# First products early, halves two blocks at once, first gates in two loads: an HGRN2 attention block with a PReLU network on one core

## The chip, the cores and the metric

The kernel runs on one core of a Trainium2 chip. A core has a matrix engine (TensorE, PE in the profile; its weight loads are listed apart, as PEld), a vector engine (VectorE, DVE), a scalar engine (ScalarE, ACT), a general engine (GpSimd, POOL) and an engine that here only issues transfers (SyncE, SP). Each works through its own queue in order and waits on semaphores that the others raise. Transfers between main memory (HBM), the on-chip memory (SBUF) and back run on 16 DMA engines that all queues share. [...]

The metric is the time of one execution on the device, in microseconds (us). A profiled execution has its own time and a span, from its first to its last instruction; the tables below and the prediction say which of these they mean.

## The reference

All is float32. With batch 4, 8 heads, 768 time steps and head width 48:

```python
f = 1 / (1 + exp(-f_logit))
state = zeros((B, H, D, D))
for t in range(S):
    state = f[:, :, t, :, None] * state + einsum('bhd,bhe->bhde', k[:, :, t], v[:, :, t])
    y[:, :, t] = einsum('bhd,bhde->bhe', q[:, :, t], state)
x = y.transpose(0, 2, 1, 3).reshape(B * S, H * D)      # 3072 x 384
h = x @ w_in                                           # 384 x 2048
g = maximum(h, 0) + alpha * minimum(h, 0)
out = g @ w_out                                        # 2048 x 384
```

So each output row of the attention is a sum over all earlier time steps of `(q . decay * k) v`, where the decay is the product of the gates `f` between the two steps. The network after it is two dense products with a PReLU between.

## The kernel before

**Tiling.** The time axis is cut into 6 chunks of 128 steps (`C`), a chunk into two halves of 64 (`CH`), those into blocks of 32 (`DB`) and those into groups of 4. Two batch elements (`U`) are worked on together. That makes 12 steps `(bp, c)`, batch pair `bp` inner and chunk `c` outer. A step's tiles hold two heads on the partitions (48 of each 64 rows, `par` 0 and 1) and batch element, head pair and time on the free axis.

**Stages of a step.** Each is a generator, and a `yield` marks where another may go on.
- `prepare` (letters P and Q; six pieces) loads `f`, `q`, `k` and `v`, takes the sigmoid (L277), and makes products: `qd` (L280, L285), `q` times the gates of 0, 1, 2 or 3 preceding steps ("lagged q"); the gates' products in a group (`kr`, `fs`), their running products (`ps`, `ss`), `k4` (L345), `us` (L312 to L342), and for whole blocks `kh`, `ks`, `q3` (L366 to L402). In steps with `c` = 0 there are also `k16` and `q16` for the pair of halves of 16 in a block of 32 (L385, L400). The sixth piece copies `q3` into `A` (L415) and, in later chunks, transposes `ks` on VectorE into `kt` (L420) and moves it with 16 transfers on SP's queue into `ksn` (L425).
- `carry` (O; two pieces) multiplies `kh` with `q3` into `off` (L442); with `c` = 0 also `k16` with `q16`, one block of 32 at a time (L452), and copies both out to `ad` (L456) and `A` (L460); with `c` = 0 TensorE transposes `ks` into `pk` (L469), copied to `ksn` (L472). The second piece multiplies `ksn` with `v` into `pd` (L482) and takes it to the carried state, which lives beside `v` in `vs` (L492, L496, or L498).
- `attend` (S) multiplies for each of the two batch elements `k` with `qd` into `raw` (L518) and `k4` with `us` into `qu` (L533), and takes the masked parts of both into `ad` by predicated copies on VectorE (L524, and L555 or L539). Then `ad` is copied into `A` (L561), `A` is multiplied with `vs` into `py` (L572), `py` is copied to `y` (L581), and `y` goes to `xT`, in the first step by products with a shifted identity (`xt`, L590, L592), later by transfers (L600).
- `network` (n) works on the 256 rows of one step: eight groups of `ph` (L614), each with the PReLU on ScalarE and VectorE (L619, L622) into `g`; then `po` (L638), copied out (L632) and stored (L634).
- The weights come as 64 bit floats and are turned to float32 in eight pieces each: a load on SP's queue into `raw` buffers (L192; four of them), upper parts on ScalarE (L197, L199; letters a and b), lead, rest and power on VectorE (L205 to L218; w and v), and a sum by a transfer that adds (L225, POOL's queue).

**What sets the order.** It is written by hand. For each pass `n` a string of letters says which generator goes on next; TensorE, VectorE and ScalarE get their instructions in exactly this order (`manual_schedule`). Pass 0 holds the first step alone, with the preparation of the second; in pass `n` the network of step `n` runs (`before`) beside the attention of step `n` + 1 and the preparation of step `n` + 2. The first four strings are in `first`, the rest of the passes use `usual`. Loads of `f`, `q` and `k` stand on POOL's queue except in the first step, where they are on SP's. A tile with one buffer is loaded anew when its last reader is done.

**PSUM.** A pool of two pairs of banks (`pair`) serves `off`, `pk`, `raw`, `qu`, `pd` and `py` in turn, a pool of four single banks (`bank`) serves `xt`, `ph` and `po`.

Of the kernel before, what the change touches and what calls it, by code (L numbers as in the profile page):

```python
# [14 lines left out]
AF = mybir.ActivationFunctionType  # L15
# [16 lines left out]
def kernel(  # L32
# [63 lines left out]
    def bank(name):  # L96
        return psn.tile([128, 512], F32, tag="net", name=name)

# [150 lines left out]
    def quads(t):  # L249
        return t.rearrange("p (n r) -> p n r", r=4)  # L250
# [5 lines left out]
    def prepare(bp, c, x):  # L256
# [5 lines left out]
        def load(name, src, bufs=2):  # L262
            t = work.tile([128, W], F32, tag=name, name=f"{name}_{i}", bufs=bufs)
            loads.dma_start(out=t.rearrange("p (u x) -> p u x", u=U),  # L264
                              in_=src[b0:b0 + U, c].rearrange("u p h t -> p u (h t)"))
            return t

        f = quads(load("f", fT, 1))
# [8 lines left out]
        nc.scalar.activation(f, f, AF.Sigmoid)  # L277
# [16 lines left out]
        yield  # L294

# [133 lines left out]

    def carry(bp, c, x):  # L430
# [3 lines left out]
        off = pair(f"off_{i}")  # L434
        for u in range(U):
            for hp in range(HP):
                for cc in range(NC2):
                    g = (u * HP + hp) * NC2 + cc
                    o = (u * HP + hp) * DB
                    for par in range(2):  # L440
                        r_ = rows(par)
                        nc.tensor.matmul(off[CH * cc:CH * cc + DB, par, o:o + DB],  # L442
                                         lhsT=kh[r_, g], rhs=q3[r_, g, 2], start=True, stop=True)
        if not c:
            for u in range(U):
                for hp in range(HP):
                    for j in range(NJ):
                        g = (u * HP + hp) * NJ + j
                        o = U * HP * DB + (u * HP + hp) * 16
                        for par in range(2):  # L450
                            r_ = rows(par)
                            nc.tensor.matmul(off[DB * j:DB * (j + 1), par, o:o + 16], lhsT=x["k16"][r_, g],  # L452
                                             rhs=x["q16"][r_, g], start=True, stop=True)
            for u in range(U):
                o = U * HP * DB + u * HP * 16
                nc.scalar.copy(ad[:, u, :, :, 16:DB], off[:, :, o:o + HP * 16].rearrange("p r (h t) -> p r h t", h=HP))  # L456
        for cc in range(NC2):
            s_ = slice(CH * cc, CH * cc + DB)
            for par in range(2):
                nc.scalar.copy(A[s_, :, par * HP:(par + 1) * HP, CH * cc + DB:CH * (cc + 1)],  # L460
                               off[s_, par, 0:U * HP * DB].rearrange("p (u h t) -> p u h t", u=U, h=HP))


        if not c:
            pk = pair(f"pk_{i}")
            for u in range(U):
                for hp in range(HP):
                    a = (u * HP + hp) * NC2
                    nc.tensor.transpose(pk[:, u, hp * 128:(hp + 1) * 128], ks[:, a:a + 2].rearrange("p c s t -> p (c s t)"), ident)  # L469
            ksn = x["ksn"] = work.tile([128, U, HP * 128], F32, tag="ksn", name=f"ksn_{i}", bufs=1)  # L470
            for u in range(U):
                nc.scalar.copy(ksn[:, u], pk[:, u])  # L472
        yield
        pd = pair(f"pd_{i}")
        ksn = x["ksn"]
        for u in range(U):
            for hp in range(HP):
                for cc in range(NC2):
                    for par in range(2):
                        o = (u * HP + hp) * D  # L480
                        s_ = halves(cc)[0]
                        nc.tensor.matmul(pd[rows(par), cc, o:o + D],  # L482
# [3 lines left out]
        def moved(cc):  # L486
# [6 lines left out]
            for par in range(2):  # L493
                now = pd[rows(par), cc, 0:U * HP * D].rearrange("p (u h e) -> p u h e", u=U, e=D)
                if c or cc:
                    nc.vector.tensor_tensor(then[:, :, par:H:2], then[:, :, par:H:2], now, ALU.add)  # L496
                else:
                    nc.scalar.copy(then[:, :, par:H:2], now)  # L498
# [5 lines left out]
    def attend(bp, c, x):  # L504

        i = f"{bp}_{c}"
        k, k4, us = (x[n] for n in ("k", "k4", "us"))


        QL, QS = (UW, UW) if c else (VW, C)  # L510
        for u in range(U):
            raw = pair(f"raw{u}_{i}")
            for hp in range(HP):
                for j in range(NJ):
                    g = (u * HP + hp) * NJ + j
                    for par in range(2):
                        r_ = rows(par)
                        nc.tensor.matmul(raw[DB * j:DB * (j + 1), par, hp * C:hp * C + QW],  # L518
                                         lhsT=k[r_, g * DB:(g + 1) * DB], rhs=qd[r_, g], start=True, stop=True)
# [8 lines left out]
            for hp in range(HP):  # L528
                for j in range(NJ):
                    g = (u * HP + hp) * NJ + j  # L530
                    for par in range(2):
                        r_ = rows(par)
                        nc.tensor.matmul(qu[DB * j:DB * (j + 1), par, hp * QS + 4:hp * QS + QL],  # L533
                                         lhsT=k4[r_, g * DB:(g + 1) * DB], rhs=us[r_, g, 4:QL], start=True, stop=True)
            if c:
# [20 lines left out]
            yield  # L556
# [49 lines left out]
    def network(bp, c, x):  # L606
# [47 lines left out]
        "P2 a P w P a P a w O P w S a w S Q a O a w S2 Q w S Q S",  # L654
        "P a w a P w2 b n2 v O n b2 v S n v n P S b S v b n S v n b v Q b n b n v O v n v Q3 S2 n2 Q2",
        "O n2 S n2 S Q S2 n3 O n Q n Q2 n S2 n Q2 n",
        "n O n2 S n2 S Q n O Q n2 S Q n S n S Q2 S Q n2",
# [78 lines left out]
```

## Time and profile before

| | us |
|---|---|
| median of 4 runs | 651.81 (649.96 to 653.48) |
| the profiled execution, its own time | 652.45 |
| its span | 650.7 |
| TensorE busy, matmuls | 607.9 |
| VectorE busy | 423.8 |
| ScalarE busy | 254.9 |
| first `ph` matmul | 51.74 |
| end of the first step's `po` | 111.28 |

The profile's page gives busy times, the span in 40 slices (16.3 us each) with the granted TensorE clock, the chain of work that ended last, and groups of instructions with the time that their engine stood idle before them and what ended it. "<-issue" after an idle time means that nothing in the profile ended it. A timeline row has start, duration, engine, line, operation, what it writes and reads, shape and count; a merged row covers several instructions. A row of a stretch has, after the stretch and its length, the busy time of PE, PEld, DVE, ACT and POOL, the granted clock (1.00 is full), the DMA engines' share and the GB/s that they moved. A matmul of float32 is counted as two instructions.

### The profile page before, as it was taken

To read this page: it belongs to the slowest core of one execution; us is meant where nothing else is said; L and a number is where in the kernel's file an instruction comes from. 1 tells how busy PE (TensorE), PEld (TensorE's weight loads), DVE (VectorE), ACT (ScalarE), POOL (GpSimd) and SP (SyncE) were. 2 spreads that over 40 slices of the span, in tenths; PEclk is the share of its full clock that TensorE was granted. 3 is DMA by queue.
4 is the path that set the end of the run, shared out by engine and by line. 5 is a ranking of instruction groups with operands and counts; after the bars stand their busy time and mean duration, and the time that the engine had idled before them with its cause. 6 is when DMAs were issued, how large, how long until landed. Compare 5 with 4: busy or idle time off the path is not lost.

```text
span 650.7 us, 17589 instructions
## 1 busy us (share of the span) xinstructions
PE 607.9 (93%) x7580; PEld 451.0 (69%) x7580; DVE 423.8 (65%) x866; ACT 254.9 (39%) x466; POOL 67.6 (10%) x114
## 2 busy tenths in 40 slices
PE   0448799999999999999999999999999999999997
PEld 0347676876876875875876876876876786786874
DVE  6879889694595686686686587577577477450220
ACT  5676782532343161361360460361351352331210
POOL 9143122000000000000000000001001000000000
PEclk9858999999999999999999999999999999999999
DMA  7989986312223213213213313313213201201000
GB/s 258 269 207 252 265 229 145 87 62 59 43 68 89 73 41 86 72 40 87 73 34 90 73 37 90 70 39 89 57 53 88 48 31 34 43 1 25 24 1 24
DMA packets 73116, 56.22 MB, mean 86 GB/s; under 512 B 47408, under 2 KB 64944, under 8 KB 73040
## 3 DMA queue, kind: packets, MB, share of 16 engines
q0 software_dynamic: 10112, 27.53, 15.9%
q1 hardware_dynamic: 57536, 25.37, 15.6%
q10 hardware_dynamic: 5392, 2.21, 1.6%
q8 instruction: 60, 0.98, 0.7%
q14 instruction: 16, 0.13, 0.1%
HBM read 36.21 MB, written 4.72 MB: 63 GB/s over the span
## 4 chain that ended last, share of the span: by engine, by line
PE 91%; DVE 4%; issue 2%; ACT 2%; DMA 1%; DVEq 0%; ACTq 0%
PE ph L614 39%; PE po L638 38%; PE py L572 3%; PE raw L518 3%; PE qu L533 3%; PE pd L482 2%; PE off L442 1%; DMA f<-in_fT 1%; PE pk L469 0%; ACT A L561 0%; PE off L452 0%; DVE us L319 0%; DVE k L345 0%; ACT us L312 0%; DVE us L342 0%
## 5 line engine op out<-in xcount | busy, mean ns | idle before, releaser
L614 PE MATMUL ph<-xT,w_in_sb 128*128 128x256 f32 x1152 | 263.6, 386 | 3.4 <-issue 3.4
L638 PE MATMUL po<-w_out_sb,g 128*128 128x384 f32 x768 | 252.9, 488 | 0.0
L614 PEld LDWEIGHTS ph<-xT,w_in_sb 128*128 128x128 f32 x1152 | 217.6, 192 | 36.9 <-issue 7.0
L638 PEld LDWEIGHTS po<-w_out_sb,g 128*128 128x128 f32 x768 | 144.9, 190 | 96.8
L622 DVE SCALAR_TENSOR_TENSOR g<-neg,om,ph 128x256 f32<-128x256 f32 x192 | 83.2, 476 | 164.3 <-ACT neg L619 164.1
L619 ACT ACTIVATE neg<-ph 128x512 f32<-128x512 f32 x96 | 57.4, 600 | 168.7 <-PE ph L614 164.2
L632 ACT COPY o<-po 128x384 f32<-128x384 f32 x24 | 11.5, 478 | 145.6 <-PE po L638 117.5
L524 DVE COPY_PREDICATED ad<-mraw,raw 128x256 f32<-128x256 int32 (+1 forms) x96 | 42.3, 441 | 7.6 <-PE raw L518 5.1
L539 DVE COPY_PREDICATED ad<-mquad,qu 128x224 f32<-128x224 int32 (+6 forms) x140 | 41.9, 299 | 6.2
L561 ACT COPY A<-ad 32x256 f32<-32x256 f32 x96 | 38.4, 400 | 2.3 <-DVE ad L539 0.9
L328 DVE TENSOR_TENSOR us<-us,fs 128x768 f32<-128x768 f32 (+5 forms) x60 | 37.2, 620 | 0.3
L312 ACT COPY us<-qd 128x256 f32<-128x256 f32 x48 | 30.2, 666 | 9.8 <-DVE qd L285 9.7
L264 POOL DMA_DIRECT2D k<-in_kT x11 | 8.3, 759 | 235.7 <-PE raw L518 208.9
L285 DVE TENSOR_TENSOR qd<-qd,f 128x768 f32<-128x768 f32 (+2 forms) x36 | 27.1, 753 | 8.2 <-ACT qd L280 8.0
L572 PEld LDWEIGHTS py<-A,vs 128*64 128x64 f32 x768 | 25.0, 145 | 10.3 <-ACT A L561 8.1
L415 ACT COPY A<-q 48x512 f32<-48x512 f32 x44 | 27.1, 616 | 9.3 <-DVE f L410 4.5
L518 PE MATMUL raw<-qd,k 48*32 48x80 f32 x1536 | 23.3, 240 | 7.9 <-issue 6.4
L572 PE MATMUL py<-A,vs 128*64 128x64 f32 x768 | 26.9, 231 | 3.9 <-ACT A L561 3.9
L518 PEld LDWEIGHTS raw<-qd,k 48*32 48x32 f32 x1536 | 18.2, 108 | 16.1 <-issue 15.4
L442 PE MATMUL off<-q,kh 48*32 48x32 f32 x768 | 9.5, 199 | 18.4 <-DVE q L366 18.4
L581 ACT COPY y<-py 128x512 f32<-128x512 f32 x24 | 12.9, 589 | 35.2 <-PE py L572 35.2
L533 PE MATMUL qu<-us,k 48*32 48x112 f32 (+1 forms) x1536 | 25.4, 259 | 0.0
(85 smaller groups left out, 437.9 us busy)
## 6 DMA issues: line engine op xcount, KB each, us to landing
w_out_raw<-in_w_out SPq DMA_DIRECT2D x8, 767.8 KB, 5.2
w_in_raw<-in_w_in SPq DMA_DIRECT2D x8, 767.2 KB, 6.0
f<-in_fT POOLq DMA_DIRECT2D x11, 512.0 KB, 4.1
q<-in_qT POOLq DMA_DIRECT2D x11, 512.0 KB, 4.0
k<-in_kT POOLq DMA_DIRECT2D x11, 512.0 KB, 4.2
out<-o SPq DMA_DIRECT2D x24, 192.0 KB, 2.0
vs<-in_v POOLq DMA_DIRECT2D x22, 192.0 KB, 3.7
w_out_sb<-w_out_lead POOLq DMA_DIRECT2D x8, 384.0 KB, 5.4
```

The lines of the kernel that those rows point to most:

```text
L312: nc.scalar.copy(q4[:, :, :, r], qdv[r][:, :, :, 0])
L328: nc.vector.tensor_tensor(us[:, :, UO[m]:UO[m] + 4 * n].rearrange("p g (i r) -> p g i r", r=4), us[:, :, skip:skip + 4 * n].rearrange("p g ...
L518: nc.tensor.matmul(raw[DB * j:DB * (j + 1), par, hp * C:hp * C + QW], lhsT=k[r_, g * DB:(g + 1) * DB], rhs=qd[r_, g], start=True, stop=True)
L524: nc.vector.copy_predicated(adu[:, :, :, d:4], mraw[:, d, :, d:4].bitcast(I32).unsqueeze(1).broadcast_to((128, H, NB, n)), rv[:, :, QO[d]: ...
L533: nc.tensor.matmul(qu[DB * j:DB * (j + 1), par, hp * QS + 4:hp * QS + QL], lhsT=k4[r_, g * DB:(g + 1) * DB], rhs=us[r_, g, 4:QL], start=Tr ...
L539: nc.vector.copy_predicated(ad[:, u, :, :, 4 * m:DB], mquad[:, lo:lo + n].bitcast(I32).unsqueeze(1).unsqueeze(1).broadcast_to((128, 2, HP, ...
L561: nc.scalar.copy(A[s_, u, :, s_], ad[s_, u].rearrange("p r h t -> p (r h) t"))
L572: nc.tensor.matmul(py[64 * par:64 * par + 64, u, o:o + CH], lhsT=vs[bp][:, cc, u, hd * D:hd * D + 64], rhs=A[:, u, par * HP + hp, CH * cc: ...
L614: nc.tensor.matmul(ph[:, j * T:(j + 1) * T], lhsT=w_in_sb[:, kt, (f + j) * 128:(f + j + 1) * 128], rhs=xT[:, kt], start=(kt == 0), stop=(k ...
L619: nc.scalar.activation(neg, phv, AF.Relu, scale=-1.0)
L622: nc.vector.scalar_tensor_tensor(g[:, j], neg[:, j], om[:, f + j:f + j + 1], phv[:, j], ALU.mult, ALU.add)
L638: nc.tensor.matmul(po[u][:, 0:DM], lhsT=gs[f // 2][:, f % 2, u * C:(u + 1) * C], rhs=w_out_sb[:, f], start=(f == 0), stop=(f == NF - 1))
```

## The change

It has four parts.

1. In the first step the load of `f` and its sigmoid are done in two halves, one for each batch element.
2. In the first step the products of `k` and lagged `q` (`raw`) move from `attend` to the end of the first piece of `prepare`, for both batch elements. `off`, `pk` and `pd` of this step take single banks in place of pairs. `attend` then does both elements' `raw` copies and `qu` products, and after them both elements' `qu` copies.
3. In steps with `c` = 0 the products of `k16` and `q16` are done for two blocks of 32 at once: half as many, each twice as wide in both directions, of which only the two diagonal blocks are used. They are copied to `ad` by eight copies in place of two.
4. The strings of the first four passes are written anew. Among other things, in the third string four pieces of the coming step's preparation are left in place of six, and the last two stand in the fourth string (its two P).

```diff
+    def two(name, begin):
+        if begin:
+            return [bank(f"{name}{k}") for k in range(2)]
+        t = pair(name)
+        return [t[:, k] for k in range(2)]
...
-        def load(name, src, bufs=2):
+        def load(name, src, bufs=2, parts=1):
             t = work.tile([128, W], F32, tag=name, name=f"{name}_{i}", bufs=bufs)
-            loads.dma_start(out=t.rearrange("p (u x) -> p u x", u=U),
-                              in_=src[b0:b0 + U, c].rearrange("u p h t -> p u (h t)"))
+            n = U // parts
+            for u in range(0, U, n):
+                loads.dma_start(out=t.rearrange("p (u x) -> p u x", u=U)[:, u:u + n],
+                                in_=src[b0 + u:b0 + u + n, c].rearrange("u p h t -> p u (h t)"))
             return t
-        f = quads(load("f", fT, 1))
+        parts = 1 if bp or c else U
+        f = quads(load("f", fT, 1, parts))
...
-        nc.scalar.activation(f, f, AF.Sigmoid)
+        for part in range(parts):
+            fp = f[:, part * W // 4 // parts:(part + 1) * W // 4 // parts]
+            nc.scalar.activation(fp, fp, AF.Sigmoid)
...
         lagged(3)
         yield
+        if not (bp or c):
+            x["raw"] = [within(i, u, k) for u in range(U)]
...
+    def within(i, u, k):
+        raw = pair(f"raw{u}_{i}")
+        for hp in range(HP):
+            for j in range(NJ):
+                g = (u * HP + hp) * NJ + j
+                for par in range(2):
+                    r_ = rows(par)
+                    nc.tensor.matmul(raw[DB * j:DB * (j + 1), par, hp * C:hp * C + QW],
+                                     lhsT=k[r_, g * DB:(g + 1) * DB], rhs=qd[r_, g], start=True, stop=True)
+        return raw
...
-                    for j in range(NJ):
-                        g = (u * HP + hp) * NJ + j
-                        o = U * HP * DB + (u * HP + hp) * 16
+                    for cc in range(NC2):
+                        g = (u * HP + hp) * NJ + 2 * cc
+                        o = at + (u * HP + hp) * DB
                         for par in range(2):
                             r_ = rows(par)
-                            nc.tensor.matmul(off[DB * j:DB * (j + 1), par, o:o + 16], lhsT=x["k16"][r_, g],
-                                             rhs=x["q16"][r_, g], start=True, stop=True)
-            for u in range(U):
-                o = U * HP * DB + u * HP * 16
-                nc.scalar.copy(ad[:, u, :, :, 16:DB], off[:, :, o:o + HP * 16].rearrange("p r (h t) -> p r h t", h=HP))
+                            nc.tensor.matmul(off[par][CH * cc:CH * (cc + 1), o:o + DB],
+                                             lhsT=x["k16"][r_, g:g + 2].rearrange("p g t -> p (g t)"),
+                                             rhs=x["q16"][r_, g:g + 2].rearrange("p g t -> p (g t)"), start=True, stop=True)
+            for par in range(2):
+                for j in range(NJ):
+                    s_ = slice(DB * j, DB * (j + 1))
+                    o = 16 * (j % 2)
+                    nc.scalar.copy(ad[s_, :, par, :, 16:DB],
+                                   off[par][s_, at:2 * at].rearrange("p (u h t) -> p u h t", u=U, h=HP)[:, :, :, o:o + 16])
...
+        if begin:
+            for stage in (first, second):
+                for u in range(U):
+                    stage(u)
+                yield
+        else:
+            for u in range(U):
+                first(u)
+                second(u)
+                yield
...
-        "P2 a P w P a P a w O P w S a w S Q a O a w S2 Q w S Q S",
-        "P a w a P w2 b n2 v O n b2 v S n v n P S b S v b n S v n b v Q b n b n v O v n v Q3 S2 n2 Q2",
-        "O n2 S n2 S Q S2 n3 O n Q n Q2 n S2 n Q2 n",
-        "n O n2 S n2 S Q n O Q n2 S Q n S n S Q2 S Q n2",
+        "P2 a P a w P2 a O w2 a O P S w S Q S a2 S w Q a w Q2 S w Q S a",
+        "b w2 n O v n S b n v S b2 v P n2 v S b v n Q b v b n S b v3 O Q n2 Q2 n S n Q S n Q",
+        "n O n2 S n2 S Q S n Q O S n3 S n Q n S n Q",
+        "n P O n2 P S n2 S Q n O Q n2 S Q n S n S Q2 S Q n2",
```

## The prediction

> **What bounds the kernel now.** I read the page first (busy shares, slices, chain), then the waits up to 79 us, then TensorE's timeline, the clock by stretch, and last the transfers behind `pd`.
>
> ```profile
> PE 607.9 (93%) x7580; PEld 451.0 (69%) x7580; DVE 423.8 (65%) x866; ACT 254.9 (39%) x466; POOL 67.6 (10%) x114
> PE   0448799999999999999999999999999999999997
> PE 91%; DVE 4%; issue 2%; ACT 2%; DMA 1%; DVEq 0%; ACTq 0%
> ```
>
> TensorE is full from the seventh slice on: after that every us by which its work starts earlier is a us of the whole, and every wait that is put into the full part is lost for good. So two questions count: when does the last product of the first step's network end (111.28 us now), and does the new order open a gap later.
>
> ```profile
> PE raw L518 <- issue: 6.4, 2, 3.8
> PE ph L614 <- issue: 3.4, 1, 3.4
> PE off L452 <- DVE us L400: 2.0, 2, 1.4
> ...
> 33.99 0.91 PE L518 MATMUL raw<-qd,k 48*32 48x80 f32 x38 [3.76 <-issue]
> 43.93 3.47 PE L572 MATMUL py<-A,vs 128*64 128x64 f32 x60 [0.35 <-ACT A L561]
> 49.07 2.83 PE L590 MATMUL xt<-y,dense 128*128 128x256 f32 x12 [1.67 <-ACT y L581]
> 77.64 9.72 PE L614 MATMUL ph<-xT,w_in_sb 128*128 128x256 f32 x36 [3.44 <-issue]
> ...
> q8 instruction: 3, 0.05, 1.2%
> ```
>
> "issue" is a wait for nothing seen. The DMA view of 23 to 39 us has three packets of a queue called instruction (the trace puts them at 24.05, 31.74 and 35.94, 16 KB each); TensorE stops at its 222nd, 349th, 476th and 1111th matmul, 127 apart or a multiple, each time with such a packet on the way or just in. So its code comes in pieces of some 127 matmuls, and a piece is asked for when the one before is entered: between entry and packet lie 0.7 to 5.2 us, then 1 us of transfer. Short matmuls (64 in 0.9 us) use up a piece sooner than that.
>
> ```profile
> 47.40:61.00 13.60, 10.48 (x233) 9.19 (x234) 13.08 (x25) 9.37 (x18) 3.51 (x5) 1.00 0.90 242
> 61.10:64.40 3.30, 3.30 (x11) 2.76 (x10) 3.20 (x7) 2.13 (x6) 2.54 (x2) 0.50 1.14 269
> 64.50:78.00 13.50, 9.93 (x288) 8.38 (x287) 11.02 (x26) 10.04 (x16) 2.48 (x3) 1.00 1.01 256
> 78.10:81.40 3.30, 3.30 (x10) 2.59 (x9) 2.63 (x6) 1.58 (x2) 0.62 (x1) 0.50 1.05 336
> ```
>
> The column before the last two is the granted clock: half (0.50) for 3.3 us after the 1.4 us wait and after the 3.4 us wait. 12 `ph` matmuls then take 4.15 us in place of 2.69, 36 take 9.72 in place of 8.07: a dip costs about 1.6.
>
> **The change, part by part** (times by the built order and the durations of this trace).
>
> *Gates by batch, `f` in two loads.* The copy L280 needs `q`, which landed at 5.90 and started at 6.29 behind the sigmoid and L278: at most 0.4 is to be had, and the second issue (0.46 on SP, before `q`, `k`, w_in) can take 0.3 back. I take -0.3 for VectorE's first chain.
>
> *`raw` early.* Its 128 matmuls run from 10.1, when `qd` is done, in TensorE's idle time before 18. That moves the code pieces: the first short piece is entered at 12, the 222nd matmul falls into L452 (20.0), the 349th into `qu` (27), and between lie the waits for ScalarE and VectorE. The stops of 2.64 and 3.76 go. On POOL the load of `k` for the second step goes from 35.37 to 16, into the busiest stretch (512 KB, some 1.4 us of all transfers); ScalarE's w_in pieces there have 3 us of slack: nothing.
>
> *Halves of 32.* 64 matmuls for 128, -0.5 on TensorE. ScalarE has 8 copies for 2 (0.43): nearest rows are 268 ns (128x128) and 362 ns (32x256) each, with overlap 0.13 to 0.36 apart: 1.0 to 2.9; I take 1.5, since the elements are 128.
>
> *Banks.* `off`, `pk` and `pd` of the first step take single banks, so that both pairs are free for `raw`. `pd` needs `off`'s banks, copied out before `ksn`, and `ph` those that L498 empties by 28: nothing.
>
> *First step, ScalarE, which now ends last.* From 20.9: 8 copies 1.5, L460 1.27, `ksn` 1.07, a w_in piece 1.9, L498 1.0, L415 1.2, the next gates 1.05 and 0.6, `qd` 1.0: 31.5. VectorE reaches the same place: 24.9, both blocks of L524 4.0, a w_in piece 1.8, first L555 0.9: 31.6. Then L561 for block 0 (1.65), two w_in pieces (3.5), L561 for block 1 (1.65), `us` (2.1), a w_in piece (1.8), `y` (1.07): 43.4, where before shows 48.93. So `xt` starts 5.5 earlier. But in before the 60 `py` at half clock (3.47) brought the clock back at 47.36, just ahead of `xt`. Now `py` is split in two, 3 us idle follow, and `xt` meets the half clock: 2.69 of work run double until the clock returns 3.4 to 6.8 us later. That costs 1.7 to 3.4 (its 2.69 and some of `ph`); I take 2.6. The first `ph` group ends at 51.6 (43.5 and twice 2.69 and 2.6, with a step for the copies; 54.43 before): **-2.8**.
>
> *Second step.* From there to the last `po` before took 56.85. The new order has, at warm rows, 7 `ph` groups (18.8), `off` 0.7, L452 0.7, `pk` 1.35, `raw` and `qu` 3.3, `pd` 0.9, `po` 20.9, `py` 2.0: 48.6. The difference, 8.25, is the stop of 3.44, the wait of 1.45, two dips and fewer L452. VectorE hardly stands still from 41 to 88 us, yet each product it gates comes 1 us or more ahead of need: block 1 of `raw` needs L524 done at 60.5 and comes up at 61.4; the last `po` accumulator needs its bank at 78 and gets it at 75; w_out pieces land 4 to 7 us ahead. Two code ends now fall into `raw` (the 730th and 857th matmul), with 5.3 and 4.2 us since the piece before against the 1.8 to 6.4 that pieces took: +1.0, and half a dip, +0.8. **-6.5**.
>
> *The later strings.* Two yields of the fourth step's preparation move out of the third pass into the fourth, behind its first and third `ph` group. The second holds the transpose `kt` (L420) and its 16 transfers on SP. In before:
>
> ```profile
> 155.33 1.25 DVE L420 STREAM_TRANSPOSE kt<-ks 128x1024 f32<-128x1024 f32 x1
> 157.24 11.74 SPq L425 DMA_DIRECT2D ksn<-kt x16
> 169.94 0.87 DVE L622 SCALAR_TENSOR_TENSOR g<-neg,om,ph 128x256 f32<-128x256 f32 x2 [1.76 <-ACT neg L619]
> 180.70 0.94 PE L482 MATMUL pd<-vs,ksn 64*48 64x48 f32 x64
> ```
>
> The pass began at 160.57, so `pd` comes 20.2 us into it; the last transfer landed at 170.24, 13.7 after `kt`'s end, 10.5 ahead of need. The first of the two yields (six VectorE instructions, 3.0 with L402 and the second L366) ends 7.2 into the pass and delays nothing: `off` reads what the first L366 made a pass earlier. But `kt` now stands on VectorE behind the gates of groups two and three, which ended 10.2 into the pass: it ends at 11.4, `ksn` lands at 25.1. TensorE waits **+5.0** at `pd` (4.0 to 5.6 by the other step's 14.3 and by all 16 issues at 0.61); behind it stand two `ph` groups and all of `po`, and nothing else fills the gap. The idle time is longer than the 3.44 that brought a dip: **+1.7** (0.9 to 2.6). In the third pass `kt` keeps 5 us of slack; the passes after are as they were.
>
> *Sum*: -2.8 - 6.5 + 6.7 = -2.6 against the profiled execution's 652.45 (its span 650.7): 649.85. That execution lies 0.64 over the median of 651.81; between the two bases I say **649.5**.
>
> [...]
>
> **Rivals.** (1) *The late `kt` is hidden.* If `pd` needed only the first transfers, or something ahead of it were as late, -9.3 alone would stand: 643. Against it: its fourth matmul reads rows of the last transfers, and SP's pitch of 0.65 is steady in three steps. (2) *Slower: code pieces stop the second step as they stopped the first.* If the two pieces at 730 and 857 take the longest seen, 7.5 (26.49 entered, 33.99 resumed), they stop TensorE for 2.2 and 3.3, with a dip each (3.2): 8.7 where I counted 1.8, so +4.3: 656.7. It decides from a loss of 4.4 on. For it: DMA is at 0.97 to 1.08 busy there. Against: most pieces took under 5. (3) *The first step isn't earlier*: ScalarE's longer queue gives back the start (8 copies at 0.36 and a w_in load late by 3): -2.8 goes: 652.7.
>
> **How the numbers follow.** Forecast 0.66, its own range 645.5 to 653.5 (the bounds of clock, code pieces and copies); rivals 0.1, 0.16, 0.08. About 0.5%, 3.3 us, is what can be told from no change. Of the forecast's share some four tenths lie below 648.5; with (1) faster is 0.36. Slower is (2) with a little of (3): 0.19. The rest is 0.45. The range 644 to 656 leaves out (1) and half of (2).
>
> **What would show it.** `raw` near 10 us and no stop of over 1 us before 40; `y` done near 43.4; `xt` taking 4 to 5.4; the last `po` of the first step's network near 102; a wait of about 5 before `pd` of the fourth step, near 172, with a half-clock stretch behind it. Wrong if `pd` doesn't wait, or if stops stand in the second step's `raw`.

## The result, and the profile after

The changed kernel is a little slower. Its median is 654.07 us over 51 runs (649.89 to 656.61), that of the kernel before 652.23 us over 79 runs (647.51 to 654.46) on the same chips. The ratio is 1.0026, with a 95% interval of 1.0017 to 1.0035. The forecast was 649.5 us, 2.3 below the median known then; the measured difference is +1.8 us. The time lies inside the range on record, and the difference is smaller than the 3.3 us that the prediction took as the least to be told from no change. But over this many runs its sign is clear, and it is the opposite of the forecast.

The profiled execution of the changed kernel took 651.21 us (span 649.3). That is 2.9 below its own median, while the profiled execution of before lay 0.2 above its own. So the two profiles by themselves show the changed kernel 1.2 us faster. This has to be kept in mind when they are read side by side, and it is settled further down.

The page of the changed kernel, as before: busy times, TensorE's slices, the shares of the chain.

```profile
PE 609.8 (94%) x7452; PEld 452.4 (70%) x7452; DVE 423.2 (65%) x866; ACT 258.9 (40%) x479; POOL 68.1 (10%) x114
PE   1549999999699999999999999999999999999997
PE 88%; SPq 1%; DMA 1%; DVE 0%; issue 0%; ACT 0%; ACTq 0%
```

TensorE has about the same amount of work (609.8 us for 607.9, with 128 counted matmuls fewer). It is full two slices sooner: the first six digits were 0, 4, 4, 8, 7 and 9 and are now 1, 5, 4, 9, 9 and 9. In exchange there is a 6 in the eleventh slice, where there was a 9, and the chain now runs through SP's queue and a transfer. Those are the two sides of the forecast, both in sight.

TensorE's timeline of the changed kernel, from its first matmul to the end of the first step's network (start, duration, engine, line, what it writes and reads, shape, count; in brackets the idle time before it and what ended it):

```profile
10.79 2.40 PE L453 MATMUL raw<-qd,k 48*32 48x80 f32 x128 [10.79 <-DVE qd L298]
20.34 1.93 PE L482 MATMUL off<-us 48*64 48x32 f32 x64 [0.56 <-DVE us L415]
...
45.40 4.67 PE L634 MATMUL xt<-y,dense 128*128 128x256 f32 x12 [3.41 <-ACT y L625]
49.91 2.75 PE L658 MATMUL ph<-xT,w_in_sb 128*128 128x256 f32 x12
...
63.88 0.69 PE L453 MATMUL raw<-qd,k 48*32 48x80 f32 x38 [0.76 <-issue]
...
91.63 10.59 PE L682 MATMUL po<-w_out_sb,g 128*128 128x384 f32 x32
```

`raw` runs at 10.79, in time in which TensorE was idle. The stops of 2.64, 3.76 and 3.44 that the profile of before had are gone; one of 0.76 is left, ahead of the 27th matmul of the second step's second `raw`. A stop there was one of the prediction's own signs of being wrong. `xt` starts 3.7 us sooner (45.40 for 49.07) and takes 4.67 for 2.83: its matmuls start 0.43 us apart up to 49.1 and 0.21 from there, and the granted clock is on record as full only from 49.13 on. The last `po` ends at 102.22, where before had 111.28.

The fourth pass of the changed kernel, by the timeline of all engines:

```profile
161.70 1.24 DVE L435 STREAM_TRANSPOSE kt<-ks 128x1024 f32<-128x1024 f32 x1
163.01 11.29 SPq L440 DMA_DIRECT2D ksn<-kt  x16
171.76 0.28 PE L516 MATMUL pd<-vs,ksn 64*48 64x48 f32 x2
177.28 1.94 PE L516 MATMUL pd<-vs,ksn 64*48 64x48 f32 x62 [5.24 <-DMA ksn<-kt]
179.16 6.96 PE L658 MATMUL ph<-xT,w_in_sb 128*128 128x256 f32 x24
```

And the stretches around it (length, busy us of PE, PEld, DVE, ACT and POOL with instruction counts, granted clock, DMA share, GB/s):

```profile
171.00:175.40 4.40, 1.04 (x6) 0.54 (x4) 4.19 (x11) 1.80 (x3) 0.69 (x1) 1.00 0.94 241
175.50:182.20 6.70, 4.92 (x69) 4.32 (x70) 5.25 (x10) 1.29 (x2) 0.00 (x0) 0.50 0.03 5
```

Two matmuls of `pd` go, the other 62 wait 5.24 us for the transfers from `kt`. Then the clock stands at half (0.50) for the whole second stretch: `pd` takes 1.94 and the 24 `ph` behind it 6.96, where before had 0.94 and 5.45:

```profile
181.57 5.45 PE L614 MATMUL ph<-xT,w_in_sb 128*128 128x256 f32 x24
```

From the pass's first `ph` (151.38) to the end of its `po` (208.97) it took 57.6 us; the same work took 49.5 before (160.41 to 209.87). That is 8.1 us lost, where the forecast had 6.7: 5.2 of wait, 2.5 of half clock, and most of the rest because the first two `pd`, cut off from the others, take 0.28 by themselves.

### The profile page after: what moved, and what is told of

Same layout as the page of the kernel before. It is cut to its first block, busy times and chain, and to the rows that moved or that the text cites. A ratio compares the mean times of both kernels' runs of the same rounds, so it can differ in the third digit from the quotient of the medians.

```text
span 649.3 us, 17338 instructions
## 1 busy us (share of the span) xinstructions
PE 609.8 (94%) x7452; PEld 452.4 (70%) x7452; DVE 423.2 (65%) x866; ACT 258.9 (40%) x479; POOL 68.1 (10%) x114
## 4 chain that ended last, share of the span: by engine, by line
PE 88%; SPq 1%; DMA 1%; DVE 0%; issue 0%; ACT 0%; ACTq 0%
PE po L682 38%; PE ph L658 38%; PE py L616 3%; PE qu L563 3%; PE raw L453 3%; PE pd L516 2%; SPq L440 1%; PE off L470 1%; DMA ksn<-kt 1%; DVE kt L435 0%; DVE g L666 0%; ACT neg L663 0%; ACT o L676 0%; ACTq L663 0%
## 5 line engine op out<-in xcount | busy, mean ns | idle before, releaser
L530 DVE TENSOR_TENSOR vs<-vs,pd 48x384 f32<-48x384 f32 x40 | 22.1, 552 | 2.5 <-PE pd L516 0.9
```

## The experiments

The kernels of one heading were timed beside the kernel before on the same chip. Ratios are to that kernel's runs.

### The two sides apart

Theory: the time is the sum of two things that have nothing to do with each other, a gain up to the end of the first step's network and a loss in the fourth pass, which comes from the late `kt` alone. Rival: the early work only runs into some other limit, so that giving back the strings brings little, or the strings alone cost little.

The changed kernel with the third and fourth strings of before:

```diff
-        "n O n2 S n2 S Q S n Q O S n3 S n Q n S n Q",
-        "n P O n2 P S n2 S Q n O Q n2 S Q n S n S Q2 S Q n2",
+        "O n2 S n2 S Q S2 n3 O n Q n Q2 n S2 n Q2 n",
+        "n O n2 S n2 S Q n O Q n2 S Q n S n S Q2 S Q n2",
```

> The changed kernel with the third and fourth strings of before, so that the transpose kt and its transfers stand in the third pass again; all else stays changed. Theory (the early steps win some 9 us, the late kt takes 8.1 of them back: 5.4 of wait at pd and 2.6 of half clock): no wait at pd of the fourth step, no half clock behind 100 us, and 8 us less than the changed kernel: 645 to 646 against its median of 654.07, ratio to before 0.987 to 0.990. Rival (the wait at pd only takes the place of another wait further on, or the early gain is given back in any case): 651 to 654, ratio near 1.

Measured: 646.35 us (642.98 to 648.87, 6 runs) beside 652.24 of before, ratio 0.990 [0.988, 0.993]. Its timeline and the same stretch of clock:

```profile
145.96 1.25 DVE L435 STREAM_TRANSPOSE kt<-ks 128x1024 f32<-128x1024 f32 x1
148.34 11.40 SPq L440 DMA_DIRECT2D ksn<-kt  x16
171.38 0.94 PE L516 MATMUL pd<-vs,ksn 64*48 64x48 f32 x64
```

```profile
160.00:175.00 15.00, 15.00 (x369) 12.80 (x351) 12.38 (x32) 6.22 (x9) 1.46 (x2) 1.00 0.33 101
175.00:190.00 15.00, 15.00 (x110) 10.10 (x108) 14.78 (x25) 5.45 (x12) 0.72 (x1) 1.00 0.11 36
```

`kt` ends 24 us ahead of `pd`; `pd` doesn't wait, TensorE is busy for 15.00 of each 15 us, and the clock is full. The kernel is faster than the one before and than the changed one.

The other way round, the kernel before with the third and fourth strings of the change:

```diff
-        "O n2 S n2 S Q S2 n3 O n Q n Q2 n S2 n Q2 n",
-        "n O n2 S n2 S Q n O Q n2 S Q n S n S Q2 S Q n2",
+        "n O n2 S n2 S Q S n Q O S n3 S n Q n S n Q",
+        "n P O n2 P S n2 S Q n O Q n2 S Q n S n S Q2 S Q n2",
```

> The kernel before with the third and fourth strings of the change, and nothing else of it. Theory (the late kt alone costs a wait and a stretch of half clock, whatever comes before): TensorE waits 5 to 5.5 at pd of the fourth step, near 181 us, the clock is at half for 3.4 to 6.8 behind it; 6.7 to 8.1 more than before: 659 to 660, ratio 1.010 to 1.0125. Rival (kt is late only because VectorE is crowded by the changed second pass): under 2 us more, ratio under 1.003.

Measured: 659.85 us (658.61 to 661.74, 6 runs), ratio 1.011 [1.009, 1.014], so +7.6. TensorE's timeline and a stretch of the clock:

```profile
186.99 1.94 PE L482 MATMUL pd<-vs,ksn 64*48 64x48 f32 x62 [4.54 <-DMA ksn<-kt]
```

```profile
186.20:192.90 6.70, 5.91 (x72) 5.05 (x73) 4.95 (x9) 1.08 (x2) 0.00 (x0) 0.50 0.01 2
```

The wait and the half clock are there, as in the changed kernel, with none of its other parts. The rival falls. The gain and the loss are separate and both large for this kernel: -5.9 and +7.6 in these runs.

### The changed kernel once more, and with one load of f

On the same chip the changed kernel was run again, to get a second profile of it.

> The changed kernel itself once more, beside the others, for a second profile. Its 51 runs fall into two kinds: 24 at a mean granted clock of 0.995 with a median of 651.99, and 22 at 0.992 with 654.76; the one profile seen is of the first kind (651.21). Theory: the second kind has one more stretch of 3.4 us at half clock, worth 1.7, in the first 80 us. Rival: the clock is the same up to 100 us and the extra stretch is behind the wait at pd. Median again 653 to 655, ratio 1.001 to 1.004.

Measured: 653.17 us (651.24 to 656.38, 12 runs), ratio 1.0018 [0.9999, 1.0037]. This time the profiled execution took 655.56 us, 4.35 more than the first. TensorE's timeline and a stretch of the clock show the difference:

```profile
45.66 5.29 PE L634 MATMUL xt<-y,dense 128*128 128x256 f32 x12 [3.42 <-ACT y L625]
...
66.00 0.69 PE L453 MATMUL raw<-qd,k 48*32 48x80 f32 x38 [1.94 <-issue]
67.20 12.31 PE L658 MATMUL ph<-xT,w_in_sb 128*128 128x256 f32 x48
...
95.44 10.59 PE L682 MATMUL po<-w_out_sb,g 128*128 128x384 f32 x32
```

```profile
67.80:71.10 3.30, 3.30 (x9) 2.62 (x8) 3.07 (x7) 1.42 (x3) 0.89 (x1) 0.50 0.84 297
```

The stop at the same matmul is 1.94 here instead of 0.76, and the half clock follows it: 48 `ph` take 12.31, where the kernel with the early `kt` takes 10.63 for them. `po` ends at 106.03 instead of 102.22. Of the 52 executions behind the result, the profiled one among them, 24 have a mean granted clock of 0.995 (median 651.99) and 22 one of 0.992 (median 654.76). The first profile has the clock 0.995 and one half-clock stretch between 50 and 200 us, the second 0.992 and two; one stretch of 3.41 at half clock is 0.0026 of the span. If the mean clock tells the two kinds apart, a good four tenths of the executions lose 2 to 3 us in this way, and the first profile came from the other kind.

The changed kernel with the first step's `f` in one load and one sigmoid:

```diff
-        parts = 1 if bp or c else U
+        parts = 1
```

> The changed kernel with f of the first step loaded and taken through the sigmoid in one piece again. In the changed profile q landed at 6.45 in place of 5.90, and VectorE's first lagged product began at 7.54 in place of 7.26. Theory (the split only delays q, k and w_in by one more issue): the first lagged product near 7.26, y 0.3 us sooner, time 0 to 0.5 less than the changed kernel. Rival (the halves bring the gates forward, as I forecast): raw 0.3 later than in the changed kernel, time 0.3 more.

Measured: 654.24 us (650.68 to 657.54, 12 runs), ratio 1.0022 [1.0004, 1.0040]: not to be told from the changed kernel. ScalarE's and TensorE's timelines:

```profile
6.25 1.04 ACT L293 COPY qd<-q 128x1024 f32<-128x1024 f32 x1
```

```profile
65.75 0.69 PE L453 MATMUL raw<-qd,k 48*32 48x80 f32 x38 [2.00 <-issue]
```

With one load the copy of `q` starts at 6.25, without waiting for `q`; with two it started at 6.47 in the first profile and had waited 0.81 for `q`. The stop in the second step is 2.00 here, and this time no half clock follows.

### Are the stops pieces of code?

The kernel before, with 32 short products (64 counted matmuls) into a spare bank ahead of the first `off`, in time in which TensorE waits:

```diff
+        if not (bp or c):
+            spare = bank("spare")
+            for n in range(32):
+                nc.tensor.matmul(spare[0:32, 0:32], lhsT=ident[0:48, 0:32], rhs=ident[0:48, 0:32], start=True, stop=True)
```

> The kernel before with 32 more short products (64 matmuls in the profile's count) of the identity into a spare bank, ahead of the first off, in TensorE's idle time before 18 us. Theory (TensorE's code comes in pieces of some 127 matmuls, and a piece that is used up before the next has landed stops it): every stop moves 64 matmuls earlier in the original order: from raw's 22nd (2.64 us in before) and the second raw's 21st (3.76) to L452's 94th and the two qu's 21st; the stop of 3.44 behind the second step's qu goes to the end of its second raw; none is left inside raw. Rival (raw waits for a bank, for qd or for a buffer): the stops of 2.64 and 3.76 stay at the same matmuls of raw. Total time within 3 of before.

One run, 653.46 us. One of the stops in the profile of before, and then TensorE's timeline here:

```profile
26.49 0.78 PE L518 MATMUL raw<-qd,k 48*32 48x80 f32 x39 [2.64 <-issue]
```

```profile
25.37 0.45 PE L456 MATMUL off<-us 48*32 48x16 f32 x33 [4.14 <-issue]
32.97 0.84 PE L537 MATMUL qu<-us,k 48*32 48x52 f32 x42 [3.71 <-issue]
37.15 0.84 PE L537 MATMUL qu<-us,k 48*32 48x52 f32 x43 [1.59 <-issue]
64.44 0.35 PE L456 MATMUL off<-us 48*32 48x16 f32 x18 [3.59 <-issue]
73.10 0.60 PE L537 MATMUL qu<-us,k 48*32 48x52 f32 x39 [1.17 <-issue]
```

The count is what stays. Before, the stops lie behind 222, 349 and 476 counted matmuls, in the first `raw`, the second `raw` and `pd`, and the one of 3.44 behind 1112. Here they lie behind 223, 350 and 477, in L456 and the two `qu`, and in the second step behind 858 and 985, in L456 and in `qu`; none is left in `raw`, and none behind 1112. (The first three are one higher than before; why is not shown.) So the stops depend on the count, not on what the products read or write.

The packets of the queue called instruction say the same. The fourteen profiles of this case hold 34 stops of over 0.3 us that nothing seen ended. 32 of them lie at such counts, 127 apart or a multiple of it, and each of these ends 1.2 to 1.6 us behind the end of a 16 KB packet on that queue. The other two lie behind 456, at `pd` in the kernel before and in the one with the late `kt`, and are left open. That the code arrives in pieces of 127 counted matmuls, and that TensorE waits for them, is shown as far as a trace can show it.

### What each part of the change is worth, with the early kt

From the faster kernel (early `kt`) one part at a time was undone. First the halves of 32, one block at a time again (128 counted matmuls in place of 64, two copies in place of eight):

```diff
-                    for cc in range(NC2):
-                        g = (u * HP + hp) * NJ + 2 * cc
+                    for j in range(NJ):
+                        g = (u * HP + hp) * NJ + j
...
-                for j in range(NJ):
-                    s_ = slice(DB * j, DB * (j + 1))
-                    o = 16 * (j % 2)
-                    nc.scalar.copy(ad[s_, :, par, :, 16:DB],
-                                   off[par][s_, at:2 * at].rearrange("p (u h t) -> p u h t", u=U, h=HP)[:, :, :, o:o + 16])
+                nc.scalar.copy(ad[:, :, par, :, 16:DB],
+                               off[par][:, at:at + U * HP * 16].rearrange("p (u h t) -> p u h t", u=U, h=HP))
```

> The changed kernel with kt early (as in the first run), and with the products of k16 and q16 done for one block of 32 at a time again: 128 matmuls of 16 columns and 2 copies of 128 partitions, in place of 64 of 32 and 8 copies of 32 partitions. In the changed profile the 64 took 1.93 us (the 128 of before 1.44) and the eight copies 2.13 (the two 0.43). Theory (two blocks at once cost more on ScalarE than they save on TensorE): y of the first step 2 us sooner, ratio to before 0.985 to 0.989, that is 1 to 3 us less than with two blocks. Rival (the copies lie beside VectorE's work, or the 64 matmuls more bring a code stop): no less than 646, ratio 0.990 or more.

Measured: 648.58 us (645.86 to 651.18, 10 runs) beside 653.11, ratio 0.995 [0.992, 0.998]. ScalarE's and TensorE's timelines:

```profile
23.32 0.44 ACT L485 COPY ad<-off 128x128 f32<-128x128 f32 x2 [1.71 <-PE off L482]
...
44.04 1.07 ACT L621 COPY y<-py 128x512 f32<-128x512 f32 x2
```

```profile
12.15 2.40 PE L453 MATMUL raw<-qd,k 48*32 48x80 f32 x128 [12.15 <-DVE qd L298]
...
21.80 1.44 PE L482 MATMUL off<-us 48*32 48x16 f32 x128 [0.55 <-DVE us L415]
...
66.41 0.69 PE L453 MATMUL raw<-qd,k 48*32 48x80 f32 x38 [2.77 <-issue]
```

In this execution `q` came late and `raw` started at 12.15. From there to `y` it took 31.9 us, while the changed kernel took 33.4 (10.79 to 44.19), so in the first step the double products and the eight copies cost 1.5: ScalarE needs 2.13 us for its eight copies and 0.44 for two. But the whole kernel is not faster for undoing them. In this execution the stop in the second step's `raw` is 2.77, and a half clock of 3.41 us follows it.

Then `raw` back in `attend`:

```diff
-        if not (bp or c):
-            x["raw"] = [within(i, u, k) for u in range(U)]
...
-            raw = x["raw"][u] if begin else within(i, u, k)
+            raw = within(i, u, k)
```

> The changed kernel with kt early, and with raw of the first step issued in attend again, its banks taken there; strings, single banks, two blocks at once and f in halves stay. Theory (issuing raw early is what takes the code stops off the first step and lets the second step's gates start): TensorE stops at code inside raw or qu before 40 us, y of the first step 2 to 5 us later than 45.3, time 648 to 651. Rival (the new strings win it alone): y within 1 us, time 645 to 647.5.

Measured: 652.73 us (649.17 to 655.87, 10 runs), ratio 1.0005 [0.9970, 1.0039]. Rows of TensorE, ScalarE and TensorE again:

```profile
35.10 1.04 PE L451 MATMUL raw<-qd,k 48*32 48x80 f32 x43 [1.72 <-issue]
```

```profile
40.65 1.66 ACT L603 COPY A<-ad 32x256 f32<-32x256 f32 x4 [3.40 <-DVE ad L587]
...
51.58 1.07 ACT L623 COPY y<-py 128x512 f32<-128x512 f32 x2
```

```profile
57.03 2.75 PE L656 MATMUL ph<-xT,w_in_sb 128*128 128x256 f32 x12
...
101.61 10.59 PE L680 MATMUL po<-w_out_sb,g 128*128 128x384 f32 x32
```

A code stop is back in `raw`, VectorE gets its products late, and ScalarE waits 3.40 for it; `y` comes at 51.58 instead of 44.30, and the first `ph` group ends at 59.78 instead of 52.68. In the whole time nothing is left of the gain (-0.4 for -5.9 against the kernel before). So with the new strings the early `raw` is worth some 7 us of the first step. It is not all of the gain: from that `ph` group to the last `po` this kernel takes 52.4 (59.78 to 112.20), the kernel before 56.8, so the second step is shorter without the early `raw` too. The new strings of the first two passes and the single banks were not undone by themselves. What shortens the second step, and whether the early `raw` would bring as much in the order of before, is not shown.

### An attempt to move the stop out of the second step

Theory: the second step loses its 2 to 3 us because a piece of code ends in its second `raw`, close behind the one before. Issuing the first element's early products twice adds 64 counted matmuls in idle time and moves every piece's end:

```diff
-            x["raw"] = [within(i, u, k) for u in range(U)]
+            x["raw"] = [within(i, u, k, 2 - u) for u in range(U)]
...
-    def within(i, u, k):
+    def within(i, u, k, times=1):
         raw = pair(f"raw{u}_{i}")
-        for hp in range(HP):
+        for hp in list(range(HP)) * times:
```

This was done to the changed kernel and to the one with the early `kt`, and the latter was run again unchanged beside them.

> The changed kernel, but the first batch element's 32 early products of k and lagged q are issued twice, with the same result: 64 more counted matmuls in time in which TensorE is idle (from 10.8 to 18). Theory (the code comes in pieces of 127 matmuls, and half of the executions lose 2 to 4 us because the 857th matmul lies in the second step's raw, 4.4 us behind the piece before): every end of a piece now lies 64 matmuls earlier in the work. In the second step the ends move to the products of k16 and q16 (near the 59th), to the first element's qu (near the 38th) and to the second element's qu (near the 25th), 5.1 to 5.3 us apart. So no stop of over 1 us in the second step, no half clock between 50 and 170 us, and a time of 651 to 652.5, about 1 to 2 less than the changed kernel's 653 to 654, with the wait before pd of the fourth step (about 5) kept. Rival (the stops belong to the second raw itself, its operands or its bank): the stop stays in the second raw at its 26th matmul and the time stays at 653 to 654.5. Second rival (the new ends are as bad, since TensorE reaches them 5 us after the piece before and pieces took up to 7.5): stops of 1 to 2.4 in qu, and 653 to 655.

> The same doubling of the first 32 early products, with the third and fourth strings of before. Theory: no stop of over 1 us in the second step, no wait at pd, no half clock after 50 us: 642 to 645, up to 2 less than the kernel with the early kt and not doubled, and a smaller spread between its runs. Rival (the stops just move to qu): 645 to 648, no less than the kernel that is not doubled.

> The changed kernel with the third and fourth strings of before, once more, beside the two kernels with doubled products on one chip. All theories: 645 to 648, about 0.990 of the kernel before. If half of its executions have a stop of 2 or more at the 26th matmul of the second raw with a stretch of half clock behind it, its runs spread over 4 us or more.

Measured, on one chip, before 652.63: the changed kernel with doubled products 657.59 us (655.29 to 658.81, 6 runs), ratio 1.0067 [1.0046, 1.0088]; the early `kt` with doubled products 648.88 (644.37 to 649.76, 6 runs), 0.9926 [0.9897, 0.9955]; the early `kt` as it was 646.62 (644.56 to 648.06, 6 runs), 0.9899 [0.9876, 0.9922]. TensorE's timeline of the first of the three:

```profile
34.17 0.84 PE L563 MATMUL qu<-us,k 48*32 48x52 f32 x43 [4.02 <-issue]
...
68.44 0.71 PE L563 MATMUL qu<-us,k 48*32 48x52 f32 x39 [2.58 <-issue]
69.08 12.11 PE L658 MATMUL ph<-xT,w_in_sb 128*128 128x256 f32 x48
```

The stops moved as the count said, out of `raw` and behind the 25th matmul of the second `qu`. The forecast of what that brings was wrong. TensorE came from the piece's entry (the first `qu`'s 38th matmul, near 61.5) to its end (65.86) in 4.4 us, not in the 5.1 to 5.3 that I had worked out, so the stop is 2.58, with the half clock behind it. New ones of 1.31 and 4.02 stand in the first step's `off` and `qu`. The profile of the early `kt` with doubled products has its stops at the same three places (0.65, 3.80 and 2.61), and that kernel too came out slower, not faster, than the one without doubling. My second rival holds: in the second step one place is as bad as the other, and in the first step the changed kernel's count was a good one.

### The best of the parts

Last, the early `kt` with `f` in one load, and the same with one block of 32 at a time (the edits are those shown above).

> The changed kernel with the third and fourth strings of before and the first step's f in one load with one sigmoid. In the four profiles seen so far with one load, the copy of q into qd starts at 6.12 to 6.25; in the eight with two loads at 5.99 to 7.91 (middle 7.1), and y follows the first raw at a fixed distance. Theory (two loads cost their start): qd's copy at 6.1 to 6.3, y done near 45.0, and 0.5 to 1.5 less than with two loads: 645 to 646, ratio 0.988 to 0.990, and a smaller spread. Rival (the start is taken up by the stop in the second raw, which ends when its packet is in, whenever TensorE comes to it): the stop is longer by as much, 2 or more, and the time is 646 to 647.5, ratio 0.990 to 0.992.

> The same, with the halves of 32 one block at a time again (128 products, two copies). Theory (the eight copies and the double products cost 1.5 in the first step, which reach the end): y done near 43.5 and 644 to 645. Rival (an earlier arrival makes the stop in the second raw longer, past 2.5, and that brings a half clock of 3.4 behind it): y near 43.5, but the stop 2.5 to 3.5 and a half clock between 66 and 72, and 646 to 649, ratio 0.991 to 0.996, not less than the first of the two.

Measured, on one chip, before 652.40: with `f` in one load 644.87 us (643.25 to 647.82, 6 runs), ratio 0.9884 [0.9860, 0.9908]; with one block as well 646.75 (645.29 to 648.85, 6 runs), 0.9914 [0.9890, 0.9938]. The first is the fastest kernel of this study, 7.5 us under before, though its interval still overlaps that of the early `kt` with two loads. TensorE's timeline of the second:

```profile
27.08 1.20 PE L512 MATMUL pd<-vs,ksn 64*48 64x48 f32 x43 [2.38 <-issue]
33.28 0.84 PE L559 MATMUL qu<-us,k 48*32 48x52 f32 x43 [3.73 <-issue]
```

That shows what the halves of 32 do. One block at a time saves the 1.5 on ScalarE and TensorE, but it has 64 more counted matmuls ahead of `qu`, and the pieces of code then end in `pd` and `qu`, where TensorE reaches them too soon: stops of 2.38 and 3.73, the second in the same place in `qu` as with the doubled products. `y` starts at 43.85 instead of 44.05, so only 0.2 of the 1.5 is left. In the earlier run with one block, with `f` in two loads, `q` came late, `raw` started 1.5 later, and the same products met no such stops. Two blocks at once came out 1.9 us faster here and some 3.4 with `f` in two loads (by the ratios to the kernel before), but the intervals overlap or touch, so it is safe to say only that the saving of 1.5 does not reach the end.

## Why the prediction was wrong, point by point

Each profile splits into two parts: up to the end of the first step's last `po`, and from there to the end.

| kernel | its time, profiled | end of that `po` | the rest |
|---|---|---|---|
| before | 652.45 | 111.28 | 541.2 |
| early `kt`, two profiles | 642.98; 646.04 | 101.89; 105.05 | 541.1; 541.0 |
| early `kt`, `f` in one load | 644.31 | 103.35 | 541.0 |
| early `kt`, late `raw` | 653.04 | 112.20 | 540.8 |
| changed, two profiles | 651.21; 655.56 | 102.22; 106.03 | 549.0; 549.5 |
| changed, `f` in one load | 652.90 | 104.09 | 548.8 |
| before, late `kt` | 661.74 | 112.62 | 549.1 |

The rest is the profiled time less the end of that `po`. It is 541.0 with the early `kt` and 549.1 with the late one, within 0.5, whatever came before. So a median says where its usual execution ends that `po`: the changed kernel at 654.07 - 549.1 = 105.0, the kernel before at 652.23 - 541.0 = 111.2. That gives -6.2 for the first part and +8.1 for the second. Their sum is the measured difference by the way they are worked out, but each was measured by itself too: with the early `kt`, where only the first part is changed, the whole time fell by 5.9 and 6.0 in two sets of runs, and with the late `kt` alone it rose by 7.6. On record stood -9.3 (-2.8 and -6.5) and +6.7.

- *The later strings, +6.7.* The mechanism was right, the place too, the size was low by 1.4. The wait is 5.24 in the first profile (4.54 to 5.24 in the five with a late `kt`) where I took 5.0; `pd` goes on 14.3 us behind the end of `kt`, as in the slower of the two steps that I had looked at. The half clock cost 2.5 (1.0 in `pd`, 1.5 in the 24 `ph`) where I took 1.7: it lasts 6.83 us after this wait, while both stretches that I took the price from in the trace of before were 3.41.
- *The first step, -2.8: too large in every profile.* I had `y` done at 43.4. It was done at 45.0 to 46.5 in the six profiles with the early `raw`, two blocks at once and no doubled products (45.26 and 45.52 in the two of the changed kernel). The first `ph` group ended at 52.66 and 53.53 where I had 51.6, so the term was -1.8 and -0.9. ScalarE's eight copies began at 22.37 and not at 20.9. Three sizes were off. The eight copies took 2.13, not 1.5. The 64 double products took 1.93 in the first step, more than the 128 single ones with 1.44, while I had -0.5. And two loads of `f` don't bring -0.3: with two, `q` landed at 5.96 to 7.89 in eight profiles, and its copy waited for it each time and started at 5.99 to 7.91 (middle 7.1); with one, `q` landed at 5.87 to 6.05 in six, before's among them, and the copy started at 6.12 to 6.31 without a wait. So the second load, put in ahead of `q`, delays it in most executions, though in two of the eight `q` was as early as with one. The whole time of the changed kernel didn't show the 0.9 (653.17 with two, 654.24 with one). So the third rival, a first step that isn't earlier, holds in part: 1.0 and 1.9 of the 2.8 are gone.
- *`xt` at half clock*: 4.67 and 5.29, as forecast (4 to 5.4). From the start of `xt` to the end of the first `ph` group it took 7.3 and 7.9, where 8.1 was reckoned. That the `py` brought the clock back in the trace of before (full from 47.36, 3.43 behind the start of their last 60) was my reading of the times; in the first profile the clock is on record as full 3.73 behind the start of `xt`.
- *The second step, -6.5.* In the first profile it was better than forecast: 49.6 from the end of the first `ph` group to the end of `po` (52.66 to 102.22), where 50.4 was reckoned (48.6 and 1.8). In the second it was 52.5 (53.53 to 106.03). So the term was -7.3 and -4.4. Of the two pieces of code that I put into `raw` only one stops TensorE: 0.41 to 2.77 us in eight profiles with the early `raw` (middle 1.6), the half clock behind it in two of those. I had counted 1.0 and half a half clock; the rival that put 2.2 and 3.3 with a half clock each there was too dark, though the second profile goes some way towards it.
- *Code in pieces.* The reasoning from the packets held in every run: the early stops were gone from the changed kernel, and 64 more matmuls moved all the stops by 64. (In the trace of before the fourth stop lies behind 1112 matmuls, one more than the prediction has, and TensorE is full from the sixth slice on, not only from the seventh; nothing hangs on either.) In the whole span 60 packets of 16 KB came with the 7580 counted matmuls of before (and as many weight loads), 59 with the 7452 of the changed kernel, one to 126. That a piece is asked for when TensorE enters the one before was my reading of the times. With the pieces counted so, the first eight packets of each of these two profiles started between 0.51 us ahead of that entry and 5.25 behind it (3.11 behind the entry at 58.44 for the one stop of the changed kernel), and TensorE stopped where it was through with the piece before the packet for the next was in.
- *The base.* The profiled execution of before was a usual one. But the changed kernel has a scatter of its own in the first 110 us (its `po` ends at 102.22, 104.09 with one load of `f`, and 106.03; with the early `kt` at 101.89 to 105.05). My forecast of 102.0 is met by two single profiles and by no median (103.9 to 105.6 by the sums above). That the first profile agreed with it to 0.2 was luck.

So the step that failed is the size of the gain, the sum of the first two terms: -9.3 on record, -6.2 in the usual execution. The late `kt` was taken 1.4 too small with it. Both errors make the change look good, and together they turn a forecast of -2.6 into the measured +1.8. How the missing 3.1 divides in the usual execution is not measured; in the two profiles the first step fell short by 1.0 and 1.9, while the second step was 0.8 better and 2.1 worse than reckoned.

## What to carry to other kernels

A gain at the head of a kernel and a loss behind it add up separately, so each has to be priced for the usual execution: take the durations of a moved chain from rows at the clock and in the company it will have, and where a stretch ends in a stop that varies, take its middle and not its best. When steps are moved to a later string, count what the last of them still has behind it: here 16 small transfers land 14 us behind the transpose that feeds them, and 8 us of the whole were lost by leaving them that late, more than the early products brought. Where TensorE stops for nothing that the profile shows, count matmuls from the start before looking for a reason in the operands; adding a few in idle time shows it in one run.

## What was not expected of the hardware

- 64 products with 64 by 32 outputs took 1.93 us in the first step, 128 with 32 by 16 outputs 1.44 in the same place; in the second step, at full clock, they take 1.14 and 1.25. The products around them (`off`, `pk`, `pd`) take 1.4 to 1.8 times as long in the first step as in the second. So the double products pay only in the second step, and 0.1 there.
- Eight copies of 32 partitions by 128 took 2.13 us, 0.27 each, two of 128 partitions by 128 took 0.44, 0.22 each: here a copy of four times the rows took no longer.
- The length of a stop alone does not tell whether the half clock follows it: it followed 1.94 in one profile, not 2.00 and 2.33 in two others, and again 2.58 and 2.77. In the profile of before it followed a wait of 1.45 for VectorE. Each stretch of half clock behind a wait lasted 3.41 or 6.83 us from the second step on, and the longer ones on record in the first step (17.07, 20.48 and 23.89) are multiples of the same 3.41.
- A kernel with 64 more matmuls in idle time, and nothing else changed, was 2.3 us slower with the early `kt` (on one chip, with intervals that overlap) and 2.7 to 3.2 with the late one (by the ratios to the kernel before). The count of matmuls ahead of a stretch of short products is a quantity of its own here.
- TensorE goes on 1.2 to 1.6 us behind the end of the packet that it waits for, in all 32 stops for code, whatever their length (0.4 to 4.1 us); in the five of the first two profiles, before and changed, 1.29 to 1.41.
